# Attention pairs taken two to a turn from the third batch on, a reordered first batch, and v of that batch through GpSimd's queue

## The chip, the core and the metric

The kernel runs on one NeuronCore of a Trainium2 chip. Its engines work side by side, each through its own instructions in order: TensorE (PE in the profile) multiplies matrices, VectorE (DVE) and ScalarE (ACT) work elementwise, GpSimd (POOL) scales v and can issue transfers, SyncE (SP) issues most transfers. Weights of a matmul are loaded by an instruction of their own (PEld). The metric is the device time of one launch in microseconds (us): 367.87 us, the median of 3 runs (367.87 to 367.97). The profiled execution took 367.07 us, of which 365.3 us are the span that the profile shows and 1.77 us lie around it.

## The reference

Softmax attention with one extra term in the denominator, then a feed-forward layer whose hidden value is the largest of three products. All arrays are float32.

```python
# q, k, v: (8, 12, 448, 64); w1, w2, w3, w_out: (768, 768)
scores = scale * np.matmul(q, k.transpose(0, 1, 3, 2))
e = np.exp(scores - m)
attn = e / (np.sum(e, axis=-1, keepdims=True) + np.exp(-m) + 1e-09)
attn_out = np.matmul(attn, v)
x = np.ascontiguousarray(attn_out.transpose(0, 2, 1, 3)).reshape(B * S, H * D)
h = np.maximum(np.maximum(x @ w1, x @ w2), x @ w3)
out = h @ w_out
```

The kernel leaves out the shift by m, which cancels: e is exp(scale * score) and the denominator is its sum plus 1.

## The kernel before

**Work and its order.** Heads are taken in pairs: 6 pairs to a batch, 48 pairs p in all. The order on every engine is the order in which the program is written out; nothing reorders it. The main loop (L452) has 49 turns. In turn `it`, the scores of pair `it` are made and the products with v of pair `it - 1`. The feed-forward work of a finished batch lies in a queue as closures, 24 or 26 of them a batch (`batch_done`): 18 *up groups* (`up_group`: six matmuls over the model dimension, then one DVE instruction that writes or takes the maximum into `hT`), then 6 or 8 *out groups* (`out_group`: six matmuls, a scaling by DVE into `o_sb`, and two stores by SP after every second). `group()` takes one out and issues it. Each turn takes 3 to 5 of them and puts them between the attention steps; `LEFT = 4` of them stay for the next batch's first turn. Before batch 0 is finished there are none, and `keep_busy(n)` puts n matmuls on a zero tile in their place (13 before the loop, 3 after the first transposes, 3 within turn 0 and 3 at the end of each of turns 0 to 4).

**One pair.** q and k of both heads lie as float32 in the tiles `raw[i]` (`qin`, `kin`, `vin` in the profile; L78), are cast to float16 by DVE (`cast_qk`) and transposed into `qkT`, for pairs 0 to 11 by eight matmuls with an identity and one DVE copy (`transposes`, L221 to L233), from pair 12 on by a transfer that SP issues (L209). v is scaled and cast by GpSimd (`scale_v`, L157) into `vst`. The 448 keys are three blocks of 128 and one of 64. `scores(p, c)` (L239) makes one block for both heads: two matmuls over only 64 of the 128 rows of the array, one in each half, which run at the same time. `scores_last` (L255) makes both heads' last 64 keys in one whole-array matmul. ACT takes the exponentials: three of 128 x 896 (L249, into `eT`) and one of 128 x 448 (L265, into `eL`). From batch 1 on, `av_main` (L273, two times three whole-array matmuls) and `av_last` (L285, two half-array matmuls side by side) give the products with v and the denominators at once, ACT forms 1/denominator as exp(-ln) (`reciprocals`, L298 and L299), and DVE multiplies (`normalize`, L307) into `xT`, the input of the up groups. In batch 0 the denominators and products are made apart (`sums_main`, `sums_last`, L316 and L325) and use `reciprocals_one` (L336, L337) and `normalize_one` (L343).

**Buffers.** In PSUM, `ps_s` has 2 buffers for scores, `ps_av` 2 for products, `ps_u` 2 for groups, fillers and transposes. `eT` has two sets by p % 2, `vst` three, `qkT` three.

**Transfers.** SP issues the loads of q, k and v, two transfers a tensor; the weights go by GpSimd's queue and are cast on the way (`load_weight`, L147): w1 in two halves in turns 3 and 4, w2, w3 and w_out in turns 5, 6 and 8. Each of SP's transfers uses one of eight semaphores in rotation, and waits for the one eight before it.

Of the kernel before, what the change touches and what calls it, by code (L numbers as in the profile page):

```python
# [21 lines left out]
def kernel(  # L22
# [44 lines left out]
    out_pool = ctx.enter_context(tc.tile_pool(name="outp", bufs=3))  # L67
# [8 lines left out]
    NRAW = 3  # L76
    HB = NPAIR // 2
# [35 lines left out]
    nc.vector.memset(raw[2][0][64:128, 0:2, NB, :], 0.0)  # L113
# [24 lines left out]
    eT = cpool.tile([128, 2, NB, 2, S], MMDT, name="eT")  # L138
# [22 lines left out]
    def casts(p):  # L161
        cast_qk(p)
        scale_v(p)

    def cast_qk(p):
        qt, kt, _ = raw[(p // HB) % NRAW]
        h0 = 2 * (p % HB)
        hs = slice(h0, h0 + 2)
        k6, q6 = k16[p % NK], q16[p % NK]
        if p == 0:  # L170

            nc.scalar.copy(out=k6[:, 0:NB], in_=kt[:, hs, 0:NB].rearrange("p h c d -> p c h d"))
            for eng, cs in ((nc.scalar.copy, slice(0, 2)), (nc.vector.tensor_copy, slice(2, NB + 1))):
                eng(out=q6[:, cs], in_=qt[:, hs, cs].rearrange("p h c d -> p c h d"))
        else:
            if p >= P_DMA and (p // NPAIR) % 2:

                nc.vector.tensor_copy(
                    out=q6[:, 1 : NB + 1], in_=qt[:, hs, 0:NB].rearrange("p h c d -> p c h d")
                )  # L180
                nc.vector.tensor_copy(out=q6[64:128, 0], in_=qt[0:64, hs, NB])
            else:
                nc.vector.tensor_copy(out=q6, in_=qt[:, hs].rearrange("p h c d -> p c h d"))  # L183
            nc.vector.tensor_copy(  # L184
                out=k6[:, 0:NB], in_=kt[:, hs, 0:NB].rearrange("p h c d -> p c h d")
            )
        for hh, half in enumerate(halves):
            last = nc.gpsimd if p == 0 else nc.vector
            last.tensor_copy(out=k6[half, NB, hh], in_=kt[0:64, h0 + hh, NB])  # L189
# [14 lines left out]
    def transposes(p):  # L204
# [10 lines left out]
        trT = ps_u.tile([128, 1024], MMDT, tag="u", name="trT")  # L215
# [32 lines left out]
    def exp_scores(p, c, stp):  # L248
        nc.scalar.activation(out=eT[:, p % 2, c], in_=stp[:, :, 0:S], func=AF.Exp, scale=scale)  # L249
# [13 lines left out]

    def exp_last(p, stl):
        nc.scalar.activation(out=eL[:, p % 2], in_=stl[:, 0, 0:S], func=AF.Exp, scale=scale)  # L265
# [3 lines left out]
    def av_main(p, hh, av=None):  # L269
        if av is None:  # L270
            av = ps_av.tile([128, 512], FP32, tag="av", name="av")
        for c in range(NB):
            nc.tensor.matmul(  # L273
                out=av[:, 0:S],
                lhsT=vst[:, p % VB, hh * NB + c, (1 - hh) * D : (3 - hh) * D],
                rhs=eT[:, p % 2, c, hh, :],
                start=(c == 0),
                stop=False,
            )
# [33 lines left out]
    def sums_main(p, ps, ones):  # L313
        for c in range(NB):
            for hh, half in enumerate(halves):
# [3 lines left out]
                    rhs=eT[:, p % 2, c, hh, :],  # L319
# [13 lines left out]
    def reciprocals_one(den):  # L333
        lnd = small.tile([128, S], FP32, tag="lnd")
        rb = small.tile([128, S], FP32, tag="rb")
        nc.scalar.activation(out=lnd, in_=den[:, 0:S], func=AF.Ln, bias=1.0)  # L336
        nc.scalar.activation(out=rb, in_=lnd, func=AF.Exp, scale=-1.0)  # L337
        return rb
# [108 lines left out]
    LEFT = 4  # L447
    keep_busy(13)
    casts(0)
    transposes(0)  # L450
    keep_busy(3)
    for it in range(NP + 1):  # L452
        p = it if it < NP else None
# [5 lines left out]
        first = {3: 1, 4: 2}.get(it)  # L459
        if first is not None:  # L460
            hs = slice(2 * first, 2 * first + 2)
            nc.vector.memset(raw[2][0][64:128, hs, NB - 1 : NB + 1, :], 0.0)
            if first == 1:
                load(NPAIR, 1, "v")
            load(NPAIR + first, 1)
        if it in (3, 4):
            load_weight(0, it - 3)
        if it in (5, 6, 8):
            load_weight((5, 6, 8).index(it) + 1)
        if it < NPAIR:  # L470

            casts(it + 1)
            for c in range(2):
                exp_scores(p, c, scores(p, c))
            if prev is None:
                keep_busy(3)
                exp_scores(p, 2, scores(p, 2))
                transposes(1)
                exp_last(p, scores_last(p))
# [12 lines left out]
            if it < NPAIR - 1:  # L492
                keep_busy(3)
            else:

                ups = [up_open()]
                up_part(ups[0], 0, 0, 0, range(3))
                av5 = ps_s.tile([128, 2, 512], FP32, tag="s", name="av5")
                sums_main(p, av5[:, 1], 1)
                sums_main(p, av5[:, 0], 0)  # L500
                sums_last(p, av5[:, 1], 1)
                sums_last(p, av5[:, 0], 0)
                rb5 = reciprocals_one(av5[:, 1])
            if prev is not None:
                normalize_one(prev, av, rb)
            if it == NPAIR - 1:
                normalize_one(p, av5[:, 0], rb5)
                batch_done(0)
        elif it == NPAIR:
            exp_scores(p, 0, scores(p, 0))  # L510

            up_part(ups[0], 0, 0, 0, (3,))
            ups.append(up_open())
            up_part(ups[1], 0, 0, 1, range(4))
            ups.append(up_open(ps_av, "av"))
            up_part(ups[2], 0, 0, 2, range(4))
            for dc in (4, 5):
                for fc, ps in enumerate(ups):
                    up_part(ps, 0, 0, fc, (dc,))
                    if dc == 5:  # L520
                        up_close(ps, 0, 0, fc)
            del queue[0:3]
            exp_scores(p, 1, scores(p, 1))
            group()
            casts(it + 1)
# [5 lines left out]
        else:  # L531
            late = it + 1 < P_DMA
            if not late:

                if it + 2 < NP:
                    cast_qk(it + 2)
                    transposes(it + 2)
                if it + 1 < NP:
                    scale_v(it + 1)
            if p is not None:  # L540
                for c in range(2):
                    exp_scores(p, c, scores(p, c))
            group()
            if late:
                casts(it + 1)
            avs = [av_main(prev, hh) for hh in range(2)]
            av_last(prev, avs)
            if p is not None:
                stp = scores(p, 2)
                stl = scores_last(p)  # L550
            rb = reciprocals(prev, avs)
            if p is not None:
                exp_scores(p, 2, stp)
                exp_last(p, stl)
# [6 lines left out]
            if it % NPAIR == 0:  # L561
                batch_done(prev // NPAIR)
# [3 lines left out]
            for _ in range(n_groups - 3):  # L566
                group()

        for n in range(NPAIR + HB, 2 * NPAIR) if it == NPAIR else (it + 5,):
            if it >= NPAIR and n < NP:  # L570
                load(n, 1)
# [32 lines left out]
```

## Time and profile before

| | |
|---|---|
| median of 3 runs | 367.87 us (367.87 to 367.97) |
| profiled execution | 367.07 us, span 365.3 us |
| instructions | 6122 |
| TensorE busy | 357.4 us, 98% of the span |
| VectorE, ScalarE, GpSimd busy | 243.4, 221.1, 53.6 us |
| read from and written to HBM | 42.47 and 11.01 MB |

How to read the profile: times are us from the span's start; L273 is line 273 of the kernel. A row of a view by time gives start, duration, engine, line, operation, output tile<-input tiles, shapes and the number of instructions in a row that are merged in it (x6); in brackets stands how long the engine was idle before, and what it waited for ("issue" is nothing that the profile shows). The duration of a matmul contains the time in which the next one already runs, so a merged row of matmuls is longer than the distance from its start to the next row's; rates are taken from starts. Rows marked POOL for a transfer are its issue, "to landing" is the time from issue until all data has arrived.

### The profile page before, as it was taken

How to read it: one execution, taken by the hardware profiler on the slowest of the kernel's cores; microseconds unless marked ns; L12 is line 12 of the kernel's file. 1: busy time of each engine (PE TensorE's matmuls, PEld its weight loads, DVE VectorE, ACT ScalarE, POOL GpSimd, SP SyncE). 2: the span in 40 equal slices, each digit the busy share in tenths (PEclk: the TensorE clock that was granted, in tenths of full speed). 3: DMA queues.
4: the chain of work that ended last, by engine and by line, in shares of the span. 5: the costliest groups of instructions: out<-in, count | busy, mean ns of one | idle time of the engine just before them, and what ended most of it. 6: DMA issues, size and time to landing. Idle time of an engine off the chain costs nothing.

```text
span 365.3 us, 6122 instructions
## 1 busy us (share of the span) xinstructions
PE 357.4 (98%) x2086; PEld 163.9 (45%) x2086; DVE 243.4 (67%) x521; ACT 221.1 (61%) x335; POOL 53.6 (15%) x159
## 2 busy tenths in 40 slices
PE   8999999999999999999999999999999999999995
PEld 3434444444444444444444444444444444445552
DVE  4474777876578677577657867757666776555553
ACT  4996476765666766666567666666566766651000
POOL 4263112211211211211121121121112112000000
PEclk9999999999999999999999999999999999999999
DMA  5999997668667888849764896758675673005006
GB/s 151 229 234 229 233 247 211 155 177 214 161 180 182 208 184 154 195 107 185 182 173 122 178 200 164 175 133 214 159 174 137 165 208 83 5 2 131 2 0 172
DMA packets 87951, 58.61 MB, mean 160 GB/s; under 512 B 43504, under 2 KB 84464, under 8 KB 87920
## 3 DMA queue, kind: packets, MB, share of 16 engines
q1 hardware_dynamic: 83632, 53.18, 59.7%
q0 software_dynamic: 3920, 4.72, 7.5%
q10 hardware_dynamic: 368, 0.33, 0.4%
q8 instruction: 16, 0.26, 0.3%
q14 instruction: 15, 0.12, 0.1%
HBM read 42.47 MB, written 11.01 MB: 146 GB/s over the span
## 4 chain that ended last, share of the span: by engine, by line
PE 91%; ACT 2%; DMA 2%; DVE 2%; issue 1%; SPq 0%; DVEq 0%
PE up L356 44%; PE op L390 15%; PE av L273 13%; PE stp L239 8%; PE stl L255 4%; PE av L285 3%; DMA kin<-in_k_dram 2%; PE busy L349 2%; ACT eT L249 1%; PE trT L221 1%; PE trT L226 1%; PE av L316 1%; DVE qkT L233 1%; DVE o_sb L415 0%; DVE qk L183 0%
## 5 line engine op out<-in xcount | busy, mean ns | idle before, releaser
L356 PE MATMUL up<-xT,w 128*128 128x448 f16 x864 | 175.3, 353 | 0.7 <-DVE xT L307 0.4
L249 ACT ACTIVATE eT<-stp 128x896 f16<-128x896 f32 x144 | 125.5, 910 | 53.3 <-PE stp L239 53.3
L356 PEld LDWEIGHTS <-w 128*128 128x128 f16 x864 | 81.7, 98 | 81.7 <-issue 12.5
L372 DVE TENSOR_TENSOR hT<-hT,up 128x448 f16<-128x448 f16 x96 | 59.6, 621 | 52.1 <-PE up L356 51.1
L157 POOL TENSOR_SCALAR vst<-vin 128x384 f16<-128x384 f32 x132 | 43.1, 338 | 255.2 <-issue 159.2
L298 ACT ACTIVATE lnd<-av 64x448 f32<-64x448 f32 x84 | 45.3, 539 | 49.0 <-PE av L285 48.0
L390 PE MATMUL op<-w,hT 128*128 128x384 f16 x336 | 59.3, 326 | 0.0
L273 PE MATMUL av<-eT,vst 128*128 128x448 f16 x252 | 54.5, 352 | 0.0
L307 DVE TENSOR_TENSOR xT<-av,rb 64x448 f16<-64x448 f32 x84 | 51.8, 617 | 1.4
L239 PE MATMUL stp<-qkT 64*128 64x448 f16 x288 | 44.1, 353 | 1.5 <-DVE qkT L233 0.7
L370 DVE CAST hT<-up 128x448 f16<-128x448 f32 x48 | 29.8, 624 | 22.9 <-PE up L356 22.2
L415 DVE TENSOR_SCALAR o_sb<-op 128x384 f32<-128x384 f32 (+1 forms) x56 | 30.8, 550 | 20.0 <-PE op L390 19.0
L390 PEld LDWEIGHTS <-hT 128*128 128x128 f16 x336 | 31.6, 98 | 24.7 <-issue 4.0
L273 PEld LDWEIGHTS <-vst 128*128 128x128 f16 x252 | 24.7, 98 | 22.4
L184 DVE CAST qk<-kin 128x384 f16<-128x384 f32 x47 | 25.7, 548 | 1.1 <-DMA kin<-in_k_dram 0.7
L265 ACT ACTIVATE eL<-stl 128x448 f16<-128x448 f32 x48 | 25.9, 539 | 0.0
L299 ACT ACTIVATE rb<-lnd 128x448 f32<-128x448 f32 x42 | 24.2, 576 | 1.3
L239 PEld LDWEIGHTS <-qkT 64*128 64x128 f16 x288 | 11.0, 94 | 23.2 <-issue 16.5
L419 ACT ACTIVATE o_sb<-op 128x192 f32<-128x192 f32 x1 | 0.3, 331 | 30.2 <-DVE o_sb L415 30.2
L189 DVE CAST qk<-kin 64x64 f16<-64x64 f32 x94 | 17.5, 187 | 1.3
L255 PE MATMUL stl<-qkT 128*128 128x448 f16 x48 | 17.4, 362 | 0.0
L285 PE MATMUL av<-eL,vst 64*128 64x448 f16 x84 | 15.2, 359 | 0.0
(50 smaller groups left out, 117.7 us busy)
## 6 DMA issues: line engine op xcount, KB each, us to landing
out_dram<-o_sb SPq DMA_DIRECT2D x54, 192.0 KB, 2.8
qin<-in_q_dram SPq DMA_DIRECT2D x46, 128.0 KB, 3.0
kin<-in_k_dram SPq DMA_DIRECT2D x45, 128.0 KB, 2.9
vin<-in_v_dram SPq DMA_DIRECT2D x44, 128.0 KB, 2.9
kin<-in_k_dram SPq DMA_DIRECT2D x46, 96.0 KB, 2.7
qin<-in_q_dram SPq DMA_DIRECT2D x45, 96.0 KB, 2.7
vin<-in_v_dram SPq DMA_DIRECT2D x44, 96.0 KB, 2.8
w<-in_moe_w_dram POOLq DMA_DIRECT2D x2, 1152.0 KB, 17.1
```

The lines of the kernel that those rows point to most:

```text
L157: nc.gpsimd.tensor_scalar(out=out, in0=in_, scalar1=LAMBDA, scalar2=1.0, op0=ALU.mult, op1=ALU.mult)
L239: nc.tensor.matmul(out=stp[:, hh, 0:S], lhsT=qkT[hh * D : hh * D + D, k0 + c * 128 : k0 + c * 128 + 128], rhs=qkT[hh * D : hh * D + D, q0 ...
L249: nc.scalar.activation(out=eT[:, p % 2, c], in_=stp[:, :, 0:S], func=AF.Exp, scale=scale)
L255: nc.tensor.matmul(out=stl[:, 0, 0:S], lhsT=qkT[:, k0 + NB * 128 : k0 + NB * 128 + 128], rhs=qkT[:, q0 : q0 + S], start=True, stop=True,)
L273: nc.tensor.matmul(out=av[:, 0:S], lhsT=vst[:, p % VB, hh * NB + c, (1 - hh) * D : (3 - hh) * D], rhs=eT[:, p % 2, c, hh, :], start=(c == ...
L298: nc.scalar.activation(out=lnd[mine], in_=avs[hh][other, 0:S], func=AF.Ln, bias=1.0)
L307: nc.vector.tensor_tensor(out=xTs[b][mine, j, :], in0=avs[hh][mine, 0:S], in1=rb[mine], op=ALU.mult)
L356: nc.tensor.matmul(out=ps[:, 0:S], lhsT=w_sb[i][:, dc, ts(fc, 128)], rhs=xTs[b][:, dc, :], start=(dc == 0), stop=(dc == NDC - 1),)
L370: nc.vector.tensor_copy(out=h, in_=ps[:, 0:S])
L372: nc.vector.tensor_tensor(out=h, in0=h, in1=ps[:, 0:S], op=ALU.max)
L390: nc.tensor.matmul(out=ps[:, 0:NW], lhsT=hTs[sb][:, fc, ts(t, 128)], rhs=wout_sb[:, fc, ts(nh, NW)], start=(fc == 0), stop=(fc == NFC - 1),)
L415: nc.vector.tensor_scalar(out=o_sb[:, cs], in0=src, scalar1=1.0 / LAMBDA, scalar2=None, op0=ALU.mult)
```

## The change

- **Pairs 12 to 47** get a loop of their own with two pairs p and p + 1 a turn, 18 turns, each with 8 to 10 groups. The order on TensorE in a turn is: `av_last(p-1)`, `scores(p, 0)`, `scores(p, 1)`, three groups, both pairs' last-block scores in one tile (`scores_last2`), one to three groups, `scores(p, 2)`, `scores(p+1, 0)`, a group, `av_main(p)`, `av_last(p)`, `scores(p+1, 1)`, `scores(p+1, 2)`, three groups, `av_main(p+1)`. ACT takes both `eL` in one instruction of 128 x 896 (`exp_last2`). q and k are cast and transposed two pairs ahead in the same turn, and one load brings q, k and v of two pairs.
- **Batch 0**: turn `it` now also makes `scores(it+1, 0)` and its exponential; the order on ACT becomes two exponentials of pair p, its `eL`, the logarithm of pair p - 1 (`log_one`), the first exponential of pair p + 1, then the reciprocal (`exp_one`). The products with v and `sums_last` come last in the turn, and `normalize_one` a turn later. `eT` has three sets. Of `keep_busy`, two times 2 in turn 0 are left behind the first 16 (20 instead of 34 matmuls). At the end of turn 5 the sums of pair 5 come first, then three up groups side by side (`ups`), with pair 6's transposes between their fourth and fifth matmul, in a `ps_s` buffer.
- **Loads**: v of pairs 0 to 5 goes by GpSimd's queue (`load_v`), between the `scale_v` of turns 0 and 1; SP's first loads are q and k alone. `raw` is four sets of two pairs instead of three of three. The first half of w1 waits for a DVE memset of one of its columns in turn 3; the other weights stand between the `scale_v` of GpSimd's order (turns 4, 5, 6, 8), and `scale_v(it)` instead of `scale_v(it+1)` stands in a turn.
- `out_pool` has 5 buffers instead of 3.

```diff
-    out_pool = ctx.enter_context(tc.tile_pool(name="outp", bufs=3))
+    out_pool = ctx.enter_context(tc.tile_pool(name="outp", bufs=5))
...
-    NRAW = 3
-    HB = NPAIR // 2
+    NRAW = 4
+    HB = 2
...
-    load(1, 1, "qk")
-    load(0, 1, "v")
-    load(2, 1, "qk")
-    load(1, 2, "v")
-    load(3, 1, "qk")
+    for n in (1, 2, 3):
+        load(n, 1, "qk")
     load(4, 2, "q")
-    load(3, 1, "v")
-    load(4, 2, "k")
-    load(4, 2, "v")
+    load(4, 1, "k")
+    load(5, 1, "k")
+
+    def load_v(p0, n_pairs):
+        load(p0, n_pairs, "v", (nc.gpsimd, nc.gpsimd))
...
-    eT = cpool.tile([128, 2, NB, 2, S], MMDT, name="eT")
+    eT = cpool.tile([128, 3, NB, 2, S], MMDT, name="eT")
...
+    def scores_last2(p):
+        stl = ps_s.tile([128, 2, 512], FP32, tag="s", name="stl")
+        for n in range(2):
+            qkT, q0, k0 = qkTs[p + n]
+            nc.tensor.matmul(
+                out=stl[:, n, 0:S],
...
+    def exp_last2(stl):
+        nc.scalar.activation(out=eL, in_=stl[:, :, 0:S], func=AF.Exp, scale=scale)
...
-    for it in range(NP + 1):
+    for it in range(P_DMA):
...
+            if it == 0:
+                cast_qk(1)
+                scale_v(0)
+                load_v(1, 1)
+                load_v(2, 2)
+                exp_scores(0, 0, scores(0, 0))
+                exp_scores(0, 1, scores(0, 1))
+                keep_busy(2)
+                exp_scores(0, 2, scores(0, 2))
+                transposes(1)
+                exp_last(0, scores_last(0))
+                keep_busy(2)
+                exp_scores(1, 0, scores(1, 0))
             else:
+                last = it == NPAIR - 1
+                if last:
+                    normalize_one(*waiting)
+                else:
+                    cast_qk(it + 1)
+                scale_v(it)
+                if it == 1:
+                    load_v(4, 2)
+                if it == 3:
+                    nc.vector.memset(w_sb[0][:, 0, 0:1], 0.0)
+                    load_weight(0, 0)
+                if waiting is not None and not last:
+                    normalize_one(*waiting)
+                exp_scores(p, 1, scores(p, 1))
                 den, av = (ps_av.tile([128, 512], FP32, tag="av", name=n) for n in ("den", "av"))
                 sums_main(prev, den, 1)
                 stp = scores(p, 2)
-                sums_main(prev, av, 0)
+                if not last:
+                    transposes(it + 1)
                 stl = scores_last(p)
                 sums_last(prev, den, 1)
-                sums_last(prev, av, 0)
                 exp_scores(p, 2, stp)
                 exp_last(p, stl)
-                rb = reciprocals_one(den)
-                transposes(it + 1)
+                lnd = log_one(den)
+                if not last:
+                    exp_scores(it + 1, 0, scores(it + 1, 0))
+                    waiting = prev, av, exp_one(lnd)
+                sums_main(prev, av, 0)
+                sums_last(prev, av, 0)
...
+    avs = [av_main(P_DMA - 1, hh) for hh in range(2)]
+    for p in range(P_DMA, NP, 2):
...
+        av_last(p - 1, avs)
+        stps = [scores(p, c) for c in range(2)]
+        rb = reciprocals(p - 1, avs)
+        for c in range(2):
+            exp_scores(p, c, stps[c])
+        group()
+        normalize(p - 1, 0, avs, rb)
+        group()
+        normalize(p - 1, 1, avs, rb)
+        if p % NPAIR == 0:
+            batch_done(p // NPAIR - 1)
+        group()
+        exp_last2(scores_last2(p))
+        if more:
+            cast_q(p + 2)
+        for _ in range(n_groups - 7):
+            group()
+        if more:
+            cast_k(p + 2)
+            transposes(p + 2)
+        scale_v(p + 1)
+        stps = [scores(p, 2), scores(p + 1, 0)]
+        exp_scores(p, 2, stps[0])
+        exp_scores(p + 1, 0, stps[1])
+        group()
+        if more:
+            cast_qk(p + 3)
+            transposes(p + 3)
+            scale_v(p + 2)
+        if p + 6 < NP:
+            load(p + 6, 2)
+        avs = [av_main(p, hh) for hh in range(2)]
+        av_last(p, avs)
+        stps = [scores(p + 1, c) for c in (1, 2)]
+        rb = reciprocals(p, avs)
+        for c in (1, 2):
+            exp_scores(p + 1, c, stps[c - 1])
+        group()
+        for hh in range(2):
+            normalize(p, hh, avs, rb)
+        group()
+        group()
+        avs = [av_main(p + 1, hh) for hh in range(2)]
```

More of the change, by code (lines that the diff above doesn't have):

```diff
@@ L508 @@
                 batch_done(0)
+                del queue[0:3]
         elif it == NPAIR:
             exp_scores(p, 0, scores(p, 0))
[L512 to L521, printed above, removed]
@@ L567 @@
                 group()
-        for n in range(NPAIR + HB, 2 * NPAIR) if it == NPAIR else (it + 5,):
-            if it >= NPAIR and n < NP:
-                load(n, 1)
+        if it == NPAIR:
+            load(10, 2)
+        if it in (8, 9):
+            load({8: 12, 9: 14}[it], 2)
+    avs = [av_main(P_DMA - 1, hh) for hh in range(2)]
+    for p in range(P_DMA, NP, 2):
+        more = p + 2 < NP
+        left = max(len(queue) - LEFT, 0)
+        to_next = (NPAIR - p % NPAIR) // 2
+        n_groups = 8 if p % NPAIR == 0 else max(8, min(10, -(-left // to_next)))
+        av_last(p - 1, avs)
+        stps = [scores(p, c) for c in range(2)]
+        rb = reciprocals(p - 1, avs)
+        for c in range(2):
+            exp_scores(p, c, stps[c])
[37 more added lines that the diff above has]
+        avs = [av_main(p + 1, hh) for hh in range(2)]
+    av_last(NP - 1, avs)
+    rb = reciprocals(NP - 1, avs)
+    group()
+    normalize(NP - 1, 0, avs, rb)
+    group()
+    normalize(NP - 1, 1, avs, rb)
+    batch_done(B - 1)
     while queue:
```

173 lines of the change are left out of this document (95 added, 78 removed).

## The prediction

> **What bounds the kernel now.** I read the page first: busy times, slices, the chain.
>
> ```profile
> PE 357.4 (98%) x2086; PEld 163.9 (45%) x2086; DVE 243.4 (67%) x521; ACT 221.1 (61%) x335; POOL 53.6 (15%) x159
> ...
> ACT  4996476765666766666567666666566766651000
> ...
> DMA  5999997668667888849764896758675673005006
> ...
> PE 91%; ACT 2%; DMA 2%; DVE 2%; issue 1%; SPq 0%; DVEq 0%
> ```
>
> A slice is 9.13 us. TensorE sets the end, but ACT is at 9 in slices 2 and 3 alone: batch 0 has another limit. So I read two stages by time. First the TensorE view of a turn of a late batch:
>
> ```profile
> 272.02 0.55 PE L239 MATMUL stp<-qkT 64*128 64x448 f16 x4
> 272.50 1.31 PE L356 MATMUL up<-xT,w 128*128 128x448 f16 x6
> 273.65 1.30 PE L273 MATMUL av<-eT,vst 128*128 128x448 f16 x6
> 274.88 0.36 PE L285 MATMUL av<-eL,vst 64*128 64x448 f16 x2
> 275.08 0.35 PE L239 MATMUL stp<-qkT 64*128 64x448 f16 x2
> 275.36 0.36 PE L255 MATMUL stl<-qkT 128*128 128x448 f16 x1
> 275.56 3.57 PE L356 MATMUL up<-xT,w 128*128 128x448 f16 x18
> 279.06 0.55 PE L239 MATMUL stp<-qkT 64*128 64x448 f16 x4
> ...
> 332.36 20.58 PE up L356 x108
> ```
>
> The last row, from the chain of waits, gives the undisturbed rate: 20.58 / 108 = 0.191 us a matmul. The turn from 272.02 to 279.06 is 7.04 us and holds 35 such slots: 24 up, 6 av, 1 stl, and four slots in which two half-array matmuls (64*128) run side by side. 35 x 0.191 = 6.67; 0.37 us are lost, and nothing is waited for. The rows say where: the six av take 1.23 instead of 1.14 before a half-array run begins, and from stp to stl there are 0.28 instead of 0.19 where it ends. A turn has two half-array runs (av_last with stp; the first two stp), so each costs 0.37 / 2 = 0.185 us. The Trainium skill, TensorEngine Tiling (Array Packing), Key Properties, says that changing the tiling mode drains TensorE; it gives no time, and the rows above are the price here.
>
> Second, ScalarE in batch 0:
>
> ```profile
> 19.39 2.53 ACT L249 ACTIVATE eT<-stp 128x896 f16<-128x896 f32 x3 [0.28 <-PE stp L239]
> 21.80 0.56 ACT L265 ACTIVATE eL<-stl 128x448 f16<-128x448 f32 x1
> 22.22 0.57 ACT L336 ACTIVATE lnd<-den 128x448 f32<-128x448 f32 x1
> 22.83 0.58 ACT L337 ACTIVATE rb<-lnd 128x448 f32<-128x448 f32 x1
> 23.69 2.53 ACT L249 ACTIVATE eT<-stp 128x896 f16<-128x896 f32 x3 [0.28 <-PE stp L239]
> ...
> 30.40 0.56 ACT L265 ACTIVATE eL<-stl 128x448 f16<-128x448 f32 x1
> ...
> 33.48 0.55 ACT L336 ACTIVATE lnd<-av 128x448 f32<-128x448 f32 x1 [1.47 <-PE av L325]
> 34.05 0.58 ACT L337 ACTIVATE rb<-lnd 128x448 f32<-128x448 f32 x1
> ```
>
> A turn is 4.30 us (23.69 - 19.39), and ACT is idle in it for 0.28 alone, waiting for the next pair's first scores. TensorE fills its gaps with fillers. At the end ACT waits 1.47 us for pair 5's sums.
>
> **The change part by part.**
>
> *Pairs 12 to 47.* No matmul is added or removed. Before, these pairs have 36 x 2 half-array runs and one more for the last av_last: 73. After, the order has three a turn (av_last with two stp; stp of both pairs; av_last with two stp): 18 x 3 + 1 = 55. 18 runs x 0.185 = 3.3 us. Bounds: 0 if merged runs drain as often as before, 18 x 0.37 = 6.7 if one run costs all that a turn loses; I take 3.3, because the loss shows at exactly the places where the mode changes.
>
> What the new order must not do is hold TensorE. Latencies after an av_last (here 274.88):
>
> ```profile
> 275.27 1.10 ACT L298 ACTIVATE lnd<-av 64x448 f32<-64x448 f32 x2 [1.13 <-PE av L285]
> 276.41 0.58 ACT L299 ACTIVATE rb<-lnd 128x448 f32<-128x448 f32 x1
> 276.89 0.90 ACT L249 ACTIVATE eT<-stp 128x896 f16<-128x896 f32 x1
> ...
> L184 DVE CAST qk<-kin 128x384 f16<-128x384 f32 x47 | 25.7, 548 | 1.1 <-DMA kin<-in_k_dram 0.7
> ...
> DMA to landing us min/median/max: 2.7/3.0/5.5
> ```
>
> With av_last at 0, ACT has rb at 2.1 and both exponentials at 3.75. Three groups end at about 4.1 (out groups: 3.6). The last-block scores then need a `ps_s` buffer, free since 2.9. Their exponential starts 0.6 after them (two slots, then 0.4 as in 275.27 - 274.88) and lasts 0.9; with 0.08 for the signal, `scores(p+1, 0)`, which needs that buffer, may go 1.58 us after them. TensorE arrives there after two slots, a group, a mode change and `scores(p, 2)`: 0.38 + 1.14 + 0.09 + 0.19 = 1.80 with an up group, 1.64 with an out group (163 ns a matmul). That passes, by 0.22 and 0.06. The second half starts at 6.2; after a group and six av its av_last is at 8.6. By the same latencies rb is ready at 10.7, the two multiplications end at 12.2 and the exponentials at 12.4; three groups later `av_main(p+1)` starts at 12.2 (out) to 12.7 (up) and needs its third block 0.38 after that. That is close too, so I charge 0.1 for all the turns together. DVE casts k of pair p + 2 after the fourth group's eviction, some 0.6 + 0.55 + 0.4 after 5.7, to 7.2; the transfer that transposes it lands 2.7 to 5.5 later (the last row), before the next turn at 13.3 to 14.0. Behind the waiting transposes on SP stand stores and loads for turns later. One load for two pairs, joined `eL` and five out buffers save work of engines that bound nothing: 0.
>
> *The passage at turn 12.* Before:
>
> ```profile
> 72.47 0.60 DVE L307 TENSOR_TENSOR xT<-av,rb 64x448 f16<-64x448 f32 x1
> ...
> 73.10 0.80 PE L239 MATMUL stp<-qkT 64*128 64x448 f16 x4
> ...
> 73.74 0.63 DVE L307 TENSOR_TENSOR xT<-av,rb 64x448 f16<-64x448 f32 x1
> ...
> 80.17 0.35 PE L356 MATMUL up<-xT,w 128*128 128x448 f16 x1 [0.37 <-DVE xT L307]
> ```
>
> Turns 11 and 12 lose some 1.0 us here: stp waits for buffers, and the first up group for `xT`. After, `av_main(11)` follows turn 11's out groups at once and needs both product buffers, the second of which is free at 74.37 with this DVE order; its second half would start at 73.4. I count 1.1 there. The wait for `xT` goes, because a third out group and the last-block scores now stand ahead of the first up group. Net +0.1.
>
> *Batch 0.* With the next pair's first scores ready, the 0.28 goes. With an exponential between lnd and rb, so does the wait of rb for lnd: they start 0.61 apart, while eL and lnd of the same size start 0.42 apart; I take 0.1. A turn is then 3.92 us. TensorE's stream keeps up: each score block waits for the exponential two before it, and its 0.5 us (signal, matmuls, start) hide under one of 0.8 (a third of 21.80 - 19.39). Four turns bring eL of pair 5 from 30.40 to 28.9. From there TensorE makes pair 4's products, pair 5's denominators and pair 5's products (three sets of six in 64-column pairs and one whole; 0.63, 0.19 and a mode change, 0.9 a set, by the second row here)
>
> ```profile
> 30.97 0.73 PE L356 MATMUL up<-xT,w 128*128 128x448 f16 x3
> 31.63 1.33 PE L316 MATMUL av<-eT,vst 128*64 128x448 f16 x12
> ...
> 33.66 3.01 PE L356 MATMUL up<-xT,w 128*128 128x448 f16 x15
> ```
>
> and starts the up groups at about 31.5, where before the dense stretch starts at 33.66 (third row). By then, however, three up matmuls, pair 6's transposes and its first scores were done, 1.3 us of work. So 2.2 - 1.3 = 0.9, and 0.3 for one half-array run less in turn 6 and shorter waits between 33.66 and 42: 1.2 us. The last reciprocal, rb of pair 5, comes at about 32 instead of 34.6, before the fifth up matmul needs it. Bounds: 2.6 (the whole advance of that reciprocal) and below 0 (next part). The 14 fillers taken out are worth nothing themselves: they lay in waits for ACT.
>
> *Loads.* Before:
>
> ```profile
> 8.44 0.51 POOL L157 TENSOR_SCALAR vst<-vin 128x384 f16<-128x384 f32 x1 [4.21 <-DMA vin<-in_v_dram]
> ...
> 19.67 1.01 POOL L147 DMA_DIRECT2D w<-in_moe_w_dram  x1
> ...
> 29.40 0.87 POOL L147 DMA_DIRECT2D w<-in_moe_w_dram  x1
> ...
> kin<-in_k_dram SPq DMA_DIRECT2D x5, 128.0 KB, 8.4
> ```
>
> The last row is of the transfers from 19 to 46 us, when the DMA engines are full. An issue costs POOL 0.9 to 1.0, so v of pairs 0 to 5 is eight issues, some 7 us on an engine that mostly waited for v; v of pair 1 is scaled at about 15 and used at 17.6. POOL then issues w1 at 19.4 to 21.3, w2 at about 22 and w3 at about 24 instead of 29.4, because v is already there. The first up group needs w1 at 31.5, w2 is needed at about 41. The load of pair 9 now waits for a memset behind three evictions, at about 36.7 instead of 33.6; with the 8.4 us of the row above k lands by 47, and is cast at 49.9. Cost 0; if either is late, 1 to 2.
>
> The Trainium skill, DMA: Bandwidth & Descriptors, SWDGE vs HWDGE vs iDMA, warns that GpSimd writes descriptors to SBUF, from which DVE locks it out in its two-port mode. By that v would come later than the issue rows say; its slack of 2.6 us covers most of it.
>
> **Sum.** 367.07 - 3.3 - 1.2 + 0.1 + 0.1 = 362.8, against the profiled execution, which lies 0.8 under the median of the runs. Forecast of the median: 363.6.
>
> **The rivals.**
>
> *A. The two-pair turn holds TensorE a little*, by 0.05 to 0.2 at the last-block exponential or the products: for it speak the margins of 0.06 and of under 0.4; against it that only out groups at the first half meet the first. 18 x 0.1 = 1.8: 365.4.
>
> *B. Slower.* Place: `scores(p+1, 0)` behind the joint exponential in all 18 turns. If that chain is longer by 0.46 with up groups (0.22 margin, then 0.24 of hold), the hold eats all 4.3 us; at 0.7 longer it is 0.48 x 18 = 8.6 against 4.3: 371.9. Against it: every piece of the chain has a row, and none is that far off.
>
> *C. Batch 0's data come late* (v, or q and k of pairs 7 to 9): TensorE, in order, waits 1 to 2 us, and ACT behind it: 365.1.
>
> *D. The merge does nothing*, the drain being paid at each change between av_last and stp, not at each run: only batch 0 is left, 366.9. Against: 274.88 to 275.08 is a plain slot of 0.20.
>
> *E. The clock falls without fillers.* The first matmuls show the price:
>
> ```profile
> 1.16 4.94 PE L349 MATMUL busy<-idle 128*128 128x448 f16 x13 [1.16 <-DVE idle L110]
> ...
> 17.62 0.39 PE L221 MATMUL trT<-ident,qk 128*128 128x128 f16 x4
> ...
> 18.07 0.73 PE L349 MATMUL busy<-idle 128*128 128x448 f16 x3
> ```
>
> 0.38 each at the start, 0.19 later. TensorE's work in a turn of batch 0 is three score slots and the last block (0.8), eight transposes (0.45, from 17.62 to 18.07), two sets of sums (1.8) and mode changes (0.4): 3.4 of 3.92 us. At half rate a turn takes 6.8; five turns add 14: 378. The Trainium skill, TensorE: Matmul & The Clock Gate, Part 1, lets the clock fall after about 3.4 us of idleness; no gap here is over 0.5.
>
> **How the numbers follow.** Forecast 0.62; A 0.15; C 0.09; B 0.07; D 0.05; E 0.02. The measurement tells 0.2% (0.7 us) from no change: faster means under 367.1. Faster: 0.62 + 0.15 + 0.08 + 0.02 of D = 0.87; same 0.04 (the rest of D and C); slower 0.09 (B, E). The range: down to 361.6 (batch 0 gives 2.6 and passage and holds cost nothing, with a little more per run); up to 366.6, which takes in A and C.
>
> **What would show it.** In the two-pair turns: three half-array runs, a pair of turns of 13.9 us where it was 14.1, no wait of stp for ACT. In batch 0: turns of 3.9, up groups dense from 31.5, full clock. Wrong would be: waits before `scores(p+1, 0)`, av or transposes in each turn, or POOL waiting for v past 17.

## The result, and the profile after

| | before | after |
|---|---|---|
| median of 6 runs | 367.92 us (367.65 to 368.36) | 364.38 us (364.02 to 365.26) |
| ratio, 95% interval | 1 | 0.9906 (0.9892 to 0.992) |
| profiled execution, span | 367.07, 365.3 us | 364.45, 362.7 us |
| instructions | 6122 | 5892 |

The kernel became faster by 3.5 us, and the time is 0.8 us over the 363.6 of the forecast. The two profiled executions lie only 2.6 us apart, because the one of before is 0.85 us below its median and the one of after 0.07 above. The steps of the sum are judged on the profiles, so against 362.8 forecast there, 1.65 us are missing. The other 0.9 us of the measured gain are in no row of the two profiles.

The page of after: busy times, slices (9.07 us each), and the shares of the chain of waits by engine.

```profile
PE 352.6 (97%) x2072; PEld 165.8 (46%) x2072; DVE 244.6 (67%) x524; ACT 219.0 (60%) x317; POOL 59.1 (16%) x167
...
ACT  4994576666566765776676666667565767660000
PEclk9999999999999999999999999999999999999999
DMA  6999999899583994689483995678665961104006
...
PE 82%; DMA 12%; POOL 2%; DVE 2%; issue 1%; ACT 0%; POOLq 0%; DVEq 0%
```

ScalarE has gone from the chain (2% before) and its full slices still end with the third; in its place transfers hold 12% (2% before). The clock stayed at 9 or more without the 14 fillers that were taken out. TensorE's view by time, of after:

```profile
31.48 2.44 PE L389 MATMUL up<-xT,w 128*128 128x448 f16 x12
...
59.11 0.54 PE L239 MATMUL trT<-ident,qk 128*128 128x128 f16 x4 [1.00 <-DVE qk L191]
...
71.60 2.31 PE L423 MATMUL op<-w,hT 128*128 128x384 f16 x12
73.90 0.73 PE L303 MATMUL av<-eT,vst 128*128 128x448 f16 x3
75.20 0.74 PE L303 MATMUL av<-eT,vst 128*128 128x448 f16 x3 [0.57 <-DVE xT L337]
75.87 0.36 PE L315 MATMUL av<-eL,vst 64*128 64x448 f16 x2
...
83.95 0.36 PE L315 MATMUL av<-eL,vst 64*128 64x448 f16 x2
...
214.15 0.36 PE L315 MATMUL av<-eL,vst 64*128 64x448 f16 x2
214.34 0.54 PE L252 MATMUL stp<-qkT 64*128 64x448 f16 x4
...
219.84 0.55 PE L252 MATMUL stp<-qkT 64*128 64x448 f16 x4
...
222.70 0.36 PE L315 MATMUL av<-eL,vst 64*128 64x448 f16 x2
...
228.03 0.36 PE L315 MATMUL av<-eL,vst 64*128 64x448 f16 x2
```

From `av_last` at 214.15 to the next turn's at 228.03 are 13.88 us for two pairs, where two turns of before took 2 x 7.04 = 14.08. The half-array matmuls (64*128) stand in three places instead of four, and no row from 214.15 to 228.03 has a bracket: nothing holds TensorE there. ScalarE in batch 0, of after:

```profile
22.98 1.90 ACT L262 ACTIVATE eT<-stp 128x896 f16<-128x896 f32 x2
...
26.91 1.90 ACT L262 ACTIVATE eT<-stp 128x896 f16<-128x896 f32 x2
28.71 0.54 ACT L295 ACTIVATE eL<-stl 128x448 f16<-128x448 f32 x1
```

A turn is 26.91 - 22.98 = 3.93 us, pair 5's eL starts at 28.71, and by the view above the up groups run from 31.48. All that TensorE waited for in after (in total, times, longest):

```profile
PE stp L252 <- DVE qkT L246: 1.4, 4, 0.4
PE busy L382 <- DVE idle L110: 1.2, 1, 1.2
PE trT L239 <- DVE qk L191: 1.0, 1, 1.0
PE av L303 <- DVE xT L337: 0.6, 1, 0.6
PE up L389 <- DMA w<-in_moe_w_dram: 0.4, 2, 0.2
PE up L389 <- DVE hT L403: 0.3, 1, 0.3
```

Before had the same waits for the idle tile and for hT, and two more lines:

```profile
PE stp L239 <- DVE qkT L233: 0.7, 4, 0.2
...
PE up L356 <- DVE xT L307: 0.4, 1, 0.4
```

New in after are the transposes (trT) that wait for a cast, av that waits for `xT`, and up groups that wait for weights. The cast itself waits, as VectorE's view by time shows, and the chain of waits (start, length) shows for what:

```profile
56.55 0.42 DVE L186 CAST qk<-qin 128x512 f16<-128x512 f32 x1
58.50 0.55 DVE L191 CAST qk<-kin 128x384 f16<-128x384 f32 x1 [1.53 <-DMA kin<-in_k_dram]
```

```profile
37.26 5.76 DMA qin<-in_q_dram
43.03 15.35 DMA kin<-in_k_dram
```

SP goes on at 37.26, when the memset lets pair 9's second half of q through; the load of pairs 10 and 11 has its last part of k issued at 43.03, when the transfer eight before it has landed (43.01), and landed at 58.38. Pair 10's k, in the same load, is wanted by the cast at about 57.0. The view of transfers between 30 and 60 us tells why 15 us pass (queues with packets, MB and share of the 16 engines' time; issues with KB and us to landing):

```profile
DMA  9999999999999999999999999999999999999999
...
q0 software_dynamic: 2941, 3.98, 74.0%
q1 hardware_dynamic: 3589, 2.96, 40.9%
...
w<-in_moe_w_out_dram POOLq DMA_DIRECT2D x1, 1152.0 KB, 27.7
```

The engines are full throughout, and GpSimd's queue (q0), with the weights, takes the larger share (the times of packets overlap). By the Trainium skill, DMA: Bandwidth & Descriptors, Queues, rings and completion order, an engine takes turns between its queues by packets; the row agrees in so far as w_out, issued at 30.24 and first used by an out group at 68.70, was moved all the while beside the loads that were wanted first.

**Where the time went.** The starts of four `av_last` on TensorE are marks at which both kernels have the same work still before them.

| | pair 6 | pair 10 | pair 12 | pair 46 | span |
|---|---|---|---|---|---|
| before | 44.87 | 70.14 | 83.31 | 322.91 | 365.28 |
| after | 44.33 | 70.91 | 83.95 | 319.97 | 362.66 |
| after against before | -0.54 | +0.77 | +0.64 | -2.94 | -2.62 |

Of the 18 half-array runs that the new order saves, one lies between pairs 10 and 12 and 17 between 12 and 46. The stretch from 12 to 46 takes 239.60 us in before and 236.02 in after, 3.58 less. Behind pair 46 after loses 0.32.

### The profile page after: what moved, and what is told of

Its sections match the earlier page's. It is cut to its first block, busy times and chain, and to the rows that moved or that the text cites. A ratio compares the mean times of both kernels' runs of the same rounds, so it can differ in the third digit from the quotient of the medians.

```text
span 362.7 us, 5892 instructions
## 1 busy us (share of the span) xinstructions
PE 352.6 (97%) x2072; PEld 165.8 (46%) x2072; DVE 244.6 (67%) x524; ACT 219.0 (60%) x317; POOL 59.1 (16%) x167
## 4 chain that ended last, share of the span: by engine, by line
PE 82%; DMA 12%; POOL 2%; DVE 2%; issue 1%; ACT 0%; POOLq 0%; DVEq 0%
PE up L389 43%; PE op L423 14%; PE av L303 12%; PE stp L252 7%; DMA kin<-in_k_dram 4%; PE av L315 3%; DMA w<-in_moe_w_dram 3%; DMA vin<-in_v_dram 3%; PE stl L282 2%; DMA qin<-in_q_dram 2%; DVE o_sb L448 1%; POOL vin L92 1%; DVE hT L403 0%; DVE xT L337 0%; POOL vst L157 0%
## 5 line engine op out<-in xcount | busy, mean ns | idle before, releaser
L389 PEld LDWEIGHTS <-w 128*128 128x128 f16 x864 | 80.4, 98 | 87.6 <-issue 17.0
L303 PE MATMUL av<-eT,vst 128*128 128x448 f16 x252 | 54.7, 352 | 0.6 <-DVE xT L337 0.6
L252 PE MATMUL stp<-qkT 64*128 64x448 f16 x288 | 41.4, 352 | 1.8 <-DVE qkT L246 1.4
L292 ACT ACTIVATE eL<-stl 128x896 f16<-128x896 f32 x18 | 16.5, 917 | 14.2 <-PE stl L282 14.2
L252 PEld LDWEIGHTS <-qkT 64*128 64x128 f16 x288 | 12.6, 94 | 20.1 <-issue 11.9
L199 DVE CAST qk<-kin 64x64 f16<-64x64 f32 x94 | 20.7, 221 | 1.2
L186 DVE CAST qk<-qin 128x512 f16<-128x512 f32 x29 | 13.2, 455 | 0.2
```

The source lines that it names most:

```text
L252: nc.tensor.matmul(out=stp[:, hh, 0:S], lhsT=qkT[hh * D : hh * D + D, k0 + c * 128 : k0 + c * 128 + 128], rhs=qkT[hh * D : hh * D + D, q0 ...
L303: nc.tensor.matmul(out=av[:, 0:S], lhsT=vst[:, p % VB, hh * NB + c, (1 - hh) * D : (3 - hh) * D], rhs=eT[:, p % 3, c, hh, :], start=(c == ...
L389: nc.tensor.matmul(out=ps[:, 0:S], lhsT=w_sb[i][:, dc, ts(fc, 128)], rhs=xTs[b][:, dc, :], start=(dc == 0), stop=(dc == NDC - 1),)
```

## The experiments

Each was compared with the kernel before on its own chip (medians 367.53 to 367.59). The times given are medians; differences from after are between medians and carry the 0.4 us by which the kernel before differs between these comparisons. Against each one's own kernel before, the gains over after are smaller by that (and the losses larger): 1.2 us for e5, 0.9 for e6, 0.15 for e7 and 1.8 for e8; e7's lies within the intervals. "Pair 12" and the like are the `av_last` starts of the profiled execution, as above.

**Is it the merged half-array runs?** `e3_four_runs` puts the two merged score blocks apart again, all else as in after:

```diff
-        stps = [scores(p, 2), scores(p + 1, 0)]
-        exp_scores(p, 2, stps[0])
-        exp_scores(p + 1, 0, stps[1])
+        exp_scores(p, 2, scores(p, 2))
         group()
+        exp_scores(p + 1, 0, scores(p + 1, 0))
```

> The changed kernel with a group put between the third scores of pair p and the first of pair p + 1, so that a two-pair turn has four half-array runs again and all else stays. Theory: 18 x 0.185 = 3.3 us more than the changed kernel, about 367.7 us, and a pair of turns of 14.08 instead of 13.88 us. Rival (the gain comes from fewer instructions on ACT and SP): within 0.5 us of the changed kernel, 364.4 us.

368.4 us, ratio 1.0023 (1.0013 to 1.0033), 4.0 us above after. TensorE's view of the same turn in it:

```profile
216.56 0.36 PE L315 MATMUL av<-eL,vst 64*128 64x448 f16 x2
...
222.25 0.36 PE L252 MATMUL stp<-qkT 64*128 64x448 f16 x2
222.55 1.31 PE L389 MATMUL up<-xT,w 128*128 128x448 f16 x6
223.79 0.36 PE L252 MATMUL stp<-qkT 64*128 64x448 f16 x2
...
230.65 0.36 PE L315 MATMUL av<-eL,vst 64*128 64x448 f16 x2
```

The turn is 14.09 us, 0.21 more than the 13.88 of after, with the same matmuls and no wait. The fourth place where the mode changes is the whole difference: 0.21 a run. From pair 12 to 46 it takes 239.62 us, as before does.

`e2_first_batch_alone` has batch 0 and the loads of after, but before's turns of one pair from pair 12 on:

```diff
-    for p in range(P_DMA, NP, 2):
+    for it in range(P_DMA, NP + 1):
...
+        if it % 2 == 0 and it + 6 < NP:
+            load(it + 6, 2)
```

> The first 12 turns as changed, pairs 12 to 47 one to a turn as before. Theory: up groups start at 31.5 us, but turn 9 waits over 1 us for k of pair 10 and turn 11 starts at about 68.2 as in the changed kernel (67.4 before), so 367.9 to 368.7 us. Rival: 366.7 us.

367.87 us, ratio 1.0012 (1.0003 to 1.0021). From pair 12 (83.96) to pair 46 (323.56) it takes 239.60 us, as before. So the first 12 turns of after, as they stand, earn nothing at all.

`e1_two_pair_alone` is the other half: before's first 12 turns, input buffers and single loads (`eT` and `out_pool` as in after), with the two-pair turns behind them:

```diff
-    for it in range(NP + 1):
+    for it in range(P_DMA):
...
+    for p in range(P_DMA, NP, 2):
...
+        for n in (p + 5, p + 6):
+            if n < NP:
+                load(n, 1)
```

> The first 12 turns as before, pairs 12 to 47 two to a turn. Theory (each merged half-array run saves 0.185 us, and what batch 0 gained was lost again to late loads in batch 1): the whole gain of the change is here, 3.3 to 3.6 us less than before, about 364.4 us. Rival (batch 0 kept its 1.2 us, the two-pair turns gave only some 2.3): 365.6 us.

373.16 us, ratio 1.0148 (1.0132 to 1.0163): slower by 5.6 us; both expectations missed. The largest wait of TensorE in it:

```profile
PE stp L261 <- DMA qkT<-qk: 6.6, 4, 2.2
```

The scores wait for transposes that SP had not issued in time, so this run says nothing against the merge; it raises the question what one load for two pairs is worth. `e9_single_loads` asks it of after itself:

```diff
-            load(p + 6, 2)
+            load(p + 6, 1)
+            load(p + 7, 1)
```

> The changed kernel with one load for each pair in place of one for two in the two-pair turns: 12 issues of 0.64 us on SP in a turn instead of 6, the same bytes. Theory (SP's issues are what made the transposes late where the two-pair turns had single loads): the transposes come up to 2.2 us late in some turns, 5 to 9 us more than the changed kernel, 370 to 373 us. Rival (those waits came from the other layout of the input buffers): 364.4 us.

371.41 us, ratio 1.0112 (1.0089 to 1.0135), 7.0 us above after. SP's view by time, of e9 and then of after (a row's duration is the time of its issues and what they stand behind):

```profile
122.86 5.42 SPq L462 DMA_DIRECT2D out_dram<-o_sb  x8
128.38 3.23 SPq L219 DMA_TRANSPOSE qkT<-qk  x2
```

```profile
119.27 5.60 SPq L462 DMA_DIRECT2D out_dram<-o_sb  x8
124.98 3.62 SPq L219 DMA_TRANSPOSE qkT<-qk  x2
```

VectorE ends the cast of k at about the same time in both (124.2 in e9, 124.5 in after); the transposes follow 0.5 us later in after and 4.2 us later in e9. Twelve issues of 0.65 us instead of six stand ahead of the eight stores: six more are 3.9 us, about the 3.7 by which the transposes come later. TensorE then waits for them:

```profile
PE stp L252 <- DMA qkT<-qk: 5.8, 4, 2.0
```

`e10_two_pair_double_loads` and `e12_two_pair_old_layout` try to give e1 that load. e10 takes the buffers of after (and so loads v of pairs 1 and 2 one by one in batch 0); e12 keeps before's sets of three pairs, in which only some pairs of loads can be joined:

```diff
-    NRAW = 3
-    HB = NPAIR // 2
+    NRAW = 4
+    HB = 2
...
-    load(1, 2, "v")
+    load(1, 1, "v")
+    load(2, 1, "v")
...
+        if p + 6 < NP:
+            load(p + 6, 2)
```

> The first 12 turns as before, but with the input buffers in four sets of two pairs, and pairs 12 to 47 two to a turn with one load for two pairs. Theory (18 merged runs of 0.21 us, and nothing from batch 0): 3.7 us less than before, 363.8 us on this scale, no wait for transposed q and k. Rival (batch 0 kept part of its gain): 365 us.

367.61 us, ratio 1.0004 (0.9992 to 1.0015); both expectations missed. The profiled execution took 368.59 us, 1.0 above the median. Pair 6's `av_last`, in before at 44.87, starts in it at 48.48: batch 0 lost 3.6 us, in which a wait of transposes for a cast is the largest single piece:

```profile
PE trT L249 <- DVE qk L185: 2.2, 1, 2.2
```

The cast waits for k of pairs 4 and 5, whose second half SP issues at 17.47, two issues of 0.65 us later than in before (16.17), and which lands at 23.62 instead of 21.18. Behind the wait the granted clock is at 0.5 for 3.4 us, which is most of the rest. That points to the two further issues on SP; a run with these issues and the old buffer sets was not made. From pair 12 to 46 e10 needs 236.34 us, 3.3 less than before.

```diff
+        if p + 6 < NP:
+            if (p + 6) % HB < HB - 1:
+                load(p + 6, 2)
+            else:
+                load(p + 6, 1)
+                load(p + 7, 1)
```

> The first 12 turns as before with the input buffers as before (three sets of three pairs), pairs 12 to 47 two to a turn with one load for two pairs wherever both lie in one set (two turns of three). Theory (each merged half-array run saves 0.21 us, single loads hurt where out groups' stores stand before a transpose, which is not the turn that has them here): 3.7 us less than before, 363.9 us on a scale where before is 367.6; from av_last of pair 11 to that of pair 47 249.2 us (252.9 before). Rival (the two-pair turns need the new first 12 turns, as the runs with two first-batch orders suggest): 366 us or more, with waits for q, k or their transposes.

365.7 us, ratio 0.9953 (0.9939 to 0.9966), between the two expectations. The first 12 turns are nearly those of before (0.36 us later at every mark from pair 6 to 10, by a wait of 0.45 us for a cast in batch 0); from pair 11 to 47 it takes 250.81 us, 1.6 more than after. Of that, 1.3 are two waits in turns 12 and 14, in TensorE's view by time:

```profile
79.82 0.36 PE L291 MATMUL stl<-qkT 128*128 128x448 f16 x1 [0.40 <-DMA qkT<-qk]
...
90.68 0.55 PE L261 MATMUL stp<-qkT 64*128 64x448 f16 x4 [0.89 <-DMA qkT<-qk]
```

From pair 16 on it is the equal of after: 212.37 against 212.36 us to pair 47. So the two-pair turns alone, on before's first batch, bring 1.9 us on the median, and the full 0.2 a turn wherever the transposes are on time.

**What did the first 12 turns lose?** Three kernels change the transfers of after. `e4_pair9_early` no longer lets pair 9's load wait for turn 6:

```diff
-        if it in (3, 5, 6):
-            p_new = {3: 7, 5: 8, 6: 9}[it]
+        for p_new in {3: (7,), 5: (8, 9)}.get(it, ()):
```

> The changed kernel with the memset and the load of pair 9 put beside those of pair 8 in turn 5, so that SP does not stand from 29 to 37 us before a memset. Theory G (this hold makes k of pair 10 late): k of pair 10 lands by about 50 us, the wait of 1.0 us in turn 9 goes, about 1.3 us less than the changed kernel, 363.1 us. Theory W (w_out, issued at 30 instead of 44 us, takes the bandwidth) and theory S (the double-size load does it): no gain from this, 364.4 us, and w2 or w3 land later.

364.6 us (five runs, 364.28 to 367.47), ratio 0.9942 (0.9906 to 0.9977): nothing gained. The transposes no longer wait, and in their place stands

```profile
PE up L389 <- DMA w<-in_moe_w_dram: 1.5, 1, 1.5
```

w2 landed at 43.03 instead of 41.91. The wait only changed its victim. `e5_w_out_later` takes something off the engines instead: w_out waits for a memset in turn 8.

```diff
+            if it == 8:
+                nc.vector.memset(w_sb[3][:, 0, 0:1], 0.0)
             load_weight((5, 6, 8).index(it) + 1)
```

> The changed kernel with the transfer of w_out held by a memset of DVE until turn 8 (about 48 us). Theory W: k of pair 10 lands some 4 us earlier, the wait in turn 9 goes, 363.1 us. Theories G and S: 364.4 us.

362.84 us, ratio 0.9878 (0.9863 to 0.9892), 1.5 us below after. w_out is issued at 49.49 instead of 30.24 and takes 14.5 us instead of 27.7; pair 10's k lands at 52.9, and its cast waits no more; from pair 8 to 9 it takes 6.36 us where after takes 7.68 and before 6.35. `e6_pair10_single` leaves w_out and puts pair 10's halves ahead of pair 11's:

```diff
-            load(10, 2)
+            load(10, 1)
+            load(11, 1)
```

> The changed kernel with pairs 10 and 11 loaded one after the other and not in one load. Theory S: q and k of pair 10 land some 4 us earlier, the wait in turn 9 goes, 363.1 us. Theories G and W: at most half of that, 363.8 to 364.4 us.

363.1 us, ratio 0.9884 (0.9869 to 0.9899), 1.3 us below after; k lands at 54.7, and from pair 8 to 9 it takes 6.35 us. Either edit alone takes the wait away: pair 10's k was late because both w_out, which was not urgent, and pair 11's share of the load went with or ahead of it through full engines.

**The passage.** `e7_both_before_group` gives pair 10's second multiplication back its place before the out group in turn 11 (in after, `av_main(11)` at 75.20 waits 0.57 us for it):

```diff
+            if it + 1 == P_DMA:
+                normalize(prev, 1, avs, rb)
             group()
-            normalize(prev, 1, avs, rb)
+            if it + 1 < P_DMA:
+                normalize(prev, 1, avs, rb)
```

> The changed kernel with both multiplications of pair 10 ahead of the last group's eviction on DVE in turn 11. Theory (the second half of av of pair 11 waits only because that multiplication stands behind an eviction): of the 1.07 us lost there 0.6 to 0.7 go, 363.7 us. Rival (the wait only moves to the next group's buffer): 364.4 us.

363.88 us, ratio 0.9899 (0.9883 to 0.9916), 0.5 us below after. TensorE's view by time in it:

```profile
74.07 1.41 PE L303 MATMUL av<-eT,vst 128*128 128x448 f16 x6
75.41 0.36 PE L315 MATMUL av<-eL,vst 64*128 64x448 f16 x2
```

The six matmuls run without a wait. From pair 10's `av_last` (71.08) to pair 11's are 4.33 us where after takes 4.96, so 0.63 us are gained, as expected; the medians alone would not show it. `e8_w_out_later_both_first` has the edits of e5 and e7 together:

```diff
+            if it == 8:
+                nc.vector.memset(w_sb[3][:, 0, 0:1], 0.0)
...
+            if it + 1 == P_DMA:
+                normalize(prev, 1, avs, rb)
```

> The changed kernel with w_out held until turn 8 and with both multiplications of pair 10 ahead of the last eviction of turn 11. Theory: the two gains are at different places and add, 1.5 + 0.5 us less than the changed kernel, 362.4 us. Rival (with w_out landing at 64 us turn 11 or pair 12's data become late): 362.8 us or more.

362.27 us, ratio 0.9866 (0.9852 to 0.988): 2.1 us below after and the fastest of all. What TensorE still waits for in it:

```profile
PE stp L252 <- DVE qkT L246: 1.7, 4, 0.6
PE busy L382 <- DVE idle L110: 1.2, 1, 1.2
PE up L389 <- DVE hT L403: 0.3, 1, 0.3
```

Against before it is 1.08 us ahead at pair 6 (43.79) and still 1.08 at pair 10 (69.06), and 1.84 at pair 12 (81.47); from there to pair 46 it takes 236.01 us, as after.

**v by GpSimd's queue.** `e11_v_by_sp` gives v of pairs 0 to 5 back to SP, in the same place of the program:

```diff
-        load(p0, n_pairs, "v", (nc.gpsimd, nc.gpsimd))
+        load(p0, n_pairs, "v", (nc.sync, nc.sync))
```

> The changed kernel with v of pairs 0 to 5 issued by SP at the same places of the program instead of by GpSimd. Theory (the DMA engines are full from 9 to 60 us, so who issues matters little): within 0.7 us of the changed kernel, 364.4 us. Rival (GpSimd's queue is what lets q and k of pairs 2 to 6 come in time; SP has 8 issues more of 0.65 us each and a wait for the eighth transfer before each): ScalarE waits in batch 0, 366 us or more.

371.43 us, ratio 1.0105 (1.0091 to 1.0118), 7.0 us above after. TensorE's and GpSimd's views by time:

```profile
20.73 1.33 PE L346 MATMUL av<-eT,vst 128*64 128x448 f16 x6 [6.52 <-POOL vst L157]
```

```profile
20.16 0.51 POOL L157 TENSOR_SCALAR vst<-vin 128x384 f16<-128x384 f32 x1 [15.88 <-DMA vin<-in_v_dram]
```

The theory missed, and the rival was right, though not by q and k: v of pair 0 is behind 24 issues on SP and is issued at 16.79 only, where GpSimd issues it at 4.30. The Trainium skill, DMA: Bandwidth & Descriptors, Rules for kernel authors, says that spreading transfers over issuing engines brings no bandwidth and only saves issue time; here the place behind 24 issues cost 7.0 us, a part of it by the clock. In before SP issues v of pair 0 among the first loads, at 5.07, and it is scaled at 8.44; such an order with the new batch 0 was not run, so the 7.0 us are not the price of SP as such.

## Why the prediction was right, and where it was not

**Pairs 12 to 47 (-3.3): right, a little too small.** The mechanism is the one named. 3.58 us came out between pairs 12 and 46, 0.211 for each of the 17 runs there against 0.185. The stretch takes 236.0 us in after, e4 to e8 and e11 alike, and 239.6 in before, e2 and e3, which have the runs. Rival D (the merge does nothing) falls with that.

**The holds (+0.1) and rivals A and B: did not happen.** A turn takes 13.88 us, 13.9 was predicted, without a wait for ScalarE. In the margins of 0.06 to 0.4 us the latencies added up from rows of before held. (B's time, by its own 8.6 us, would be 372.2 and not 371.9.)

**Batch 0 (-1.2): nearly every mark was hit, and the gain was lost to late data.** ScalarE's turn is 3.93 us (3.92 predicted), eL of pair 5 comes at 28.71 (28.9), the up groups at 31.48 (31.5). Yet at pair 6 after is only 0.54 ahead, and at pair 12 it is 0.64 behind, where -1.2, the passage's +0.1 and one of the 18 runs (-0.2) were forecast: 1.9 us are missing there. e8, in which no weight and no cast of pair 10 is waited for, is 1.08 ahead at pairs 6 and 10: the term itself stood within 0.1.

**Loads (0): the step that failed.** It asked of v, w1, w2 and pair 9's k whether each lands in time. v of pair 1 is scaled at 13.74 (15), and pair 9's load goes on at 37.26 (36.7). But "POOL waiting for v past 17", one of its own signs of being wrong, did happen: v of pair 2 comes at 17.65 and that of pair 4 at 23.73. No matmul waits for v, but w2 stands behind it in GpSimd's order and is issued at 24.71 instead of about 22. The weights then come just too late: the first up group starts 0.05 us after w1's first half has landed (31.43) and 0.47 us behind the matmul before it (0.20 in e8), the second half costs 0.2 and w2 0.2, together about the 0.5 that lie between after and e8 at pair 6. These waits differ between the kernels with this first batch, from none in e8 and e9 to 1.5 in e4.

The larger part is a load that the step did not ask about: pair 10's k was wanted at 57.0 and came too late, and turn 9 lost 1.3 us. The row that it went by, 8.4 us to landing for 128 KB, was that of before with pairs loaded singly; with pairs 10 and 11 in one load, and w_out beside it from 30 instead of 44 us, the landing takes 15 for 192 KB. Rival C named the place (q or k of a later pair, 1 to 2 us) for pairs 7 to 9, and it happened for pair 10. e5 and e6 show the cause from two sides.

**"One load for two pairs ... : 0": right as a price, wrong as a reason.** It costs nothing, but it does not merely save work of an engine that bounds nothing. SP's issue time is bound to the transposes, and without that edit the kernel would have been 7.0 us slower (e9), more than all that the change gains.

**The passage (+0.1): right.** Twelve out matmuls from 71.60 end at 73.56 (12 x 0.163), the products start at 73.90 and reach `av_last` at 75.87 after 1.97 us instead of 1.23: 0.34 + 0.74 = 1.1 us lost, as counted. From pair 10 to 12 after takes 0.13 us less than before, and with the one run saved there (0.21) the passage cost 0.08 net. e7 takes 0.6 back, by the order of two steps, which the prediction had taken as given.

**Clock (rival E): did not happen**, at a mean granted clock of 0.998. That the mechanism exists is seen in e11: behind its idle time of 6.52 us six matmuls take 1.33 us, where before twelve took as much, and the mean clock is 0.990. The Trainium skill, TensorE: Matmul & The Clock Gate, Part 1, lets the clock fall after about 3.4 us of idleness; here less was enough. In e1 and e10 the granted clock is at 0.5 for 3.41 us behind waits of 1.88 and 2.23 us, and every stretch of clock between two changes in e1, e10 and e11 is a multiple of 3.41 us. Cut into such steps, the traces show the clock at 0.5 after each step with 1.88 us of idleness or more, and at 1 after each with 1.72 or less; e9 waits for 2.01 us at one place and keeps its clock, because 0.98 and 1.03 of them fall into two steps. The waits of after, at most 1.0 us once the first matmuls have run, cost no clock.

**The sum, and some luck.** On the profiles, against 362.8: first 12 turns +1.9, main term -0.46, holds -0.1, the end +0.3, together 1.7 of the 1.65 missing (the terms are rounded). The +0.3 is in no term. In after, 24 out matmuls from 325.34 would be through at 329.25; the first up matmul starts at 329.56, 0.05 us after VectorE has emptied the third of these four out groups, behind the second multiplication of pair 47. It needs that buffer, `ps_u` having two, so the order on VectorE very likely costs the 0.3. The median came within 0.8 of the forecast although 1.65 are missing on the profiles: the profile of before lay 0.85 under its median, as the forecast assumed of after too, and that of after lay 0.07 over its own. That half of the miss is hidden in this way is luck. Still open are what these 0.85 us are and 0.3 of e12's 1.6 us.

## What to carry to other kernels

Where TensorE is full, count the places where its mode changes: bringing half-array matmuls together is worth 0.2 us for each run saved, if the buffers and latencies around it still fit. When an early stage is made faster, list every transfer that comes after it with the time at which it will now be wanted, and ask of each large transfer that is not urgent whether it runs beside an urgent one; holding w_out back was worth 1.2 to 1.5 us for one memset. And price an edit that "only saves issues" by what stands behind them in their queue, not by the share of busy time of their engine.

## What the runs showed of the hardware

- Bringing half-array matmuls (64*128) together saves 0.21 us for each run of them that goes (3.58 us for 17 runs, e3: 14.09 instead of 13.88 us a turn).
- The granted clock was decided in steps of 3.41 us: a step with 1.88 us of idle TensorE or more (e1, e10, e11) was followed by half the clock, one with up to 1.72 us (e1, e9) was not.
- Between 30 and 60 us the transfers have all 16 engines full in after, and up to about 58 us in before. There an earlier issue of one transfer made another late (e4: w2 by 1.1 us); what helped was less work at that time (e5) or the urgent pair first (e6).
- The time to landing of the same kind of load goes from 8.4 us (k, 128 KB, in before) to 15.35 us (k, 192 KB, beside pair 11's and w_out). With w_out moved to 49.49, its own falls from 27.7 to 14.5 us.
- An issue on SP takes 0.6 us, and one on GpSimd of v 0.61 to 0.80 us, less than the 0.9 to 1.0 of the weights' issues that the prediction went by. In these eight issues no sign was seen of GpSimd being kept from them while VectorE was busy.
